# Chunked attention and a GELU layer on one core: zero products in TensorE's waits of the first tile, a weight cast moved, and three mm1 blocks taken by halves of K

## The chip, the cores and the metric

The kernel runs on one core of a Trainium2 chip. The metric is the device time of one execution in microseconds; smaller is better. The kernel before was timed in three runs: 282.14, 281.04 and 281.98 us, with a median of 281.98 us. A further execution was profiled; its own time was 281.53 us.

## The reference

```python
def _attn_ref(q, k, v):                       # (8, 8, 576, 64) float32
    chunk = 64
    nc = S // chunk
    scale = 1.0 / np.sqrt(D)
    # q, k, v in chunks of 64 rows; attention inside each chunk only
    scores = scale * np.matmul(q_c, k_c.transpose(0, 1, 2, 4, 3))
    ...
    attn = attn / (np.sum(attn, axis=-1, keepdims=True) + 1e-09)
    out = np.matmul(attn, v_c)
    ...

def _moe_ref(x, w_in, w_out):                 # x (4608, 512)
    h = x @ w_in                              # w_in (512, 2048)
    g = 0.5 * h * (1.0 + erf(h * inv_sqrt2))
    return (g @ w_out).astype(np.float32)     # w_out (2048, 512)
```

The attention output of all heads, laid side by side, is x (4608 rows of 512). The output is float32.

## The kernel before

The 4608 rows are cut into nine tiles of 512. Tiles 0 to 7 are the first eight chunks of each batch; the ninth gathers the last chunk of all eight batches. For each tile the kernel computes attention, which gives x transposed (512 features in four groups `ks` of 128 partitions by 512 rows, bf16), then mm1 (16 blocks `f` of 128 columns of w_in, each four products over `ks`, then GELU on ScalarE into `h`), then mm2 (`h` times w_out). The attention of a tile is computed on TensorE between the mm2 products of the tile before. From tile 3 on mm2 uses seven half-size products in the place of eight.

The order of the instructions on each engine is the order of the program text: the kernel stands in a manual schedule, and an engine takes its instructions in that order and waits for what each needs. All loads are issued by SyncE, in text order. They arrive as float32 in five `stage` buffers (two `wsum` buffers for some of the weights) and are cast to bf16 by DVE (`DV`), ScalarE (`AC`) or GpSimd (`PO`). The order of loads at the start is q and k of tile 0 by groups of two heads, v of tile 0, w_in in four blocks of 512 columns (the first two in two parts each), and then w_out, with q, k and v of tile 1 between.

The change lies in the first tile, where nothing runs beside the attention:

- `T[0]` to `T[7]` (`att_T`, line 162) transpose q and k of the four head groups on TensorE, q and k in turn, and copy them out of PSUM (q by DVE, k by ScalarE). `transposed` (line 155) takes a bank of `ps_tp` for q and of `ps_mm` for k.
- `att_S(0, g)` (line 363) makes the scores of a group in `ps_at` banks and their exponentials on ScalarE.
- `att_sums` (line 375) and `att_spread` (line 387) make the row sums with short products and spread the reciprocals, with a reciprocal and a transpose on DVE for each group.
- `att_av` (line 404) multiplies by v, first groups 0 and 1 (`g2` = 0) for half of the row blocks, then for the other half, then groups 2 and 3 (`g2` = 1). `att_x` (line 415) scales the result into x on DVE.
- `keep_warm(n)` (line 688) issues n products of 512 columns on zeros (`rest`) into a `ps_mm` bank of its own. It is called with a count of 7 at the start and of 3 behind `T[1]`, and four times with a count of 1; the diff touches the last four.
- `mm1_begin(0, 3)` (line 451) makes the first three blocks of mm1: blocks 0 and 1 by halves of K, then block 2 whole. Blocks 0 to 3 of w_in are cast by `win[0](i, engine)` (line 671).

After that, `phase(0, ...)` (line 623) runs the other mm1 blocks of tile 0, then its mm2 with the attention of tile 1 between: `duo_S`, `duo_sums`, `duo_av` (line 350, which needs v of tile 1, cast by GpSimd in `cast_v_plain`) and `duo_x` (line 357). Tile 1's mm1 follows.

Of the kernel before, what the change touches and what calls it, by code (L numbers as in the profile page):

```python
# [11 lines left out]
def kernel(  # L12
# [9 lines left out]
    nc = tc.nc  # L22
    P = 128
    f32 = mybir.dt.float32
# [4 lines left out]
    CH = 64  # L29
# [7 lines left out]
    CT = NC - 1  # L37
    MT = CT * CH
    NT = B + 1
    KS = d_model // P  # L40
# [5 lines left out]
    rest = consts.tile([P, 512], bf16, name="rest")  # L46
# [30 lines left out]
    ps_tp = ctx.enter_context(tc.tile_pool(name="ps_tp", bufs=2, space=bass.MemoryType.PSUM))  # L77
    ps_at = ctx.enter_context(tc.tile_pool(name="ps_at", bufs=3, space=bass.MemoryType.PSUM))
# [8 lines left out]
    tiles = [dict() for _ in range(NT)]  # L87
# [52 lines left out]
    def cast_v_plain(t, copy, ns=range(CT // 2), hs=slice(0, H)):  # L140
        st = tiles[t]
        if 0 in ns:
            st["v"] = ld.tile([P, H, CT // 2, D], bf16, tag="v", name="v_nat")
        for n in ns:
            copy(st["v"][:, hs, n], st["vf"][:, hs, n])
# [5 lines left out]
    def cast_qk(t, nm, g, copy):  # L151
        st = tiles[t]
        copy(st[nm][:, g].rearrange("p j r d -> p r j d"), st[nm + "f"][:, 2 * g:2 * g + 2])  # L153

    def transposed(t, nm, g):
        pool, tag = (ps_tp, "tp") if t or nm == "q" else (ps_mm, "mm")
        tp = pool.tile([P, 2, J, P], bf16, tag=tag, name="tp")
        for j in range(J):
            nc.tensor.transpose(tp[:, 0, j], tiles[t][nm][:, g, j].rearrange("p r d -> p (r d)"), ident[:])  # L159
        return tp[:, 0].rearrange("p j (i c) -> p i c j", i=CT)  # L160

    def att_T(t, nm, g, copy):
        tp = transposed(t, nm, g)
        if (nm, "T") not in tiles[t]:
            tiles[t][nm, "T"] = hsum.tile([P, G, CT, CH], bf16, tag=f"s{1 + 2 * t + (nm == 'q')}", name=nm + "T")
        xT = tiles[t][nm, "T"][:, g]
        copy(xT.rearrange("p i (c j) -> p i c j", j=J), tp)
        tiles[t][nm + "T", g] = xT

    def parity_blocks(ns=range(4)):  # L170

        for n in ns:
            for a in range(2):
                for r in range(2):
                    c = a ^ r
                    yield n, r, c, 2 * n + c, slice(CH * r, CH * (r + 1)), slice(CH * c, CH * (c + 1))
# [186 lines left out]
    def att_S(t, g):  # L363

        st = tiles[t]
        if g % 2 == 0:
            st["s_ps"] = [ps_at.tile([P, 2, CT // 2, CH], f32, tag="at", name="s_ps") for _ in range(2)]
        for n, r, c, i, rs, cs in parity_blocks():
            nc.tensor.matmul(st["s_ps"][r][cs, g % 2, n], st["kT", g][rs, i, :], st["qT", g][rs, i, :],
                             start=True, stop=True, tile_position=(CH * r, CH * c))  # L370
        st["pT", g] = work.tile([P, 2, CT // 2, CH], bf16, tag="pT", name="pT", bufs=8)
        for r in range(2):
            nc.scalar.activation(st["pT", g][:, r], st["s_ps"][r][:, g % 2], Act.Exp, scale=scale)

    def att_sums(t, g):

        st = tiles[t]
        pT = st["pT", g]
        st["sums", g] = ps_mm.tile([P, CT // 2, 2, 2], f32, tag="mm", name="sums_ps")
        for n in range(CT // 2):  # L380
            for e in range(2):
                for s in range(G):
                    nc.tensor.matmul(st["sums", g][QD * s:QD * (s + 1), n, :, e],
                                     pT[:, s // 2, n, 32 * e:32 * (e + 1)], ones_r[:],
                                     start=True, stop=True, tile_position=(0, QD * s))

    def att_spread(t, g):

        st = tiles[t]
        if g % 2 == 0:  # L390
            st["rcs", g // 2] = hsum.tile([P, 2, MT], f32, tag=f"s{3 + g // 2}", name="rcs")
        r1 = work.tile([P, NB], f32, tag="r1", name="r1", bufs=2)
        nc.vector.reciprocal(r1[:], st["sums", g][:].rearrange("p n c e -> p (n c e)"))
        nc.vector.transpose(st["rcs", g // 2][:, g % 2].rearrange("p (n e) -> p n e", e=32),  # L394
                            r1[:].to_broadcast([P, NB, 32]))

    def att_rc(t, g):
# [3 lines left out]
        nc.vector.transpose(rc[:], rb[:, g].to_broadcast([P, NB, 32]))  # L401
        tiles[t]["rc", g] = rc

    def att_av(t, g2, ns):

        st = tiles[t]
        pool, tag = ((ps_tp, "tp"), (ps_at, "at"))[g2]
        if 0 in ns:
            st["av", g2] = [pool.tile([P, 2, CT // 2, CH], f32, tag=tag, name="av_ps") for _ in range(2)]
        for g in (2 * g2, 2 * g2 + 1):  # L410
            for n, r, c, i, rs, cs in parity_blocks(ns):
                nc.tensor.matmul(st["av", g2][c][rs, g % 2, n], st["v"][cs, 2 * g + r, n, :], st["pT", g][cs, r, n],
                                 start=True, stop=True, tile_position=(CH * c, CH * r))

    def att_x(t, g2, c, ns):

        st = tiles[t]
        def part(p):
            return p.rearrange("p g (n c e) -> p g n c e", c=2, e=CH)[:, :, ns[0]:ns[-1] + 1, c]
        nc.vector.tensor_tensor(part(st["x"][:, 2 * g2:2 * g2 + 2]), st["av", g2][c][:, :, ns[0]:ns[-1] + 1],  # L420
                                part(st["rcs", g2][:]), op=mybir.AluOpType.mult)

    NB = MT // 32
    DV, AC, PO = nc.vector.tensor_copy, nc.scalar.copy, nc.gpsimd.tensor_copy

    def att_units(t, cq=DV, ck=DV):
        tiles[t]["x"] = xpool.tile([P, G, MT], bf16, tag="x", name="x")
        T = []
        for g in range(G):
            T += [lambda g=g: att_T(t, "q", g, cq),  # L430
                  lambda g=g: att_T(t, "k", g, ck if t == 0 or g < 2 else DV)]
        return T


# [16 lines left out]
    def mm1_begin(t, n):  # L451

        st = tiles[t]
        st["h"] = hpool.tile([P, FF, MT], bf16, tag="h", name="h")
        h_ps = [ps_mm.tile([P, MT], f32, tag="mm", name="h_ps") for _ in range(n)]
        order = [(f, ks) for k2 in range(2) for f in range(n - 1) for ks in (2 * k2, 2 * k2 + 1)] + \
                [(n - 1, ks) for ks in range(KS)]
        for f, ks in order:
            nc.tensor.matmul(h_ps[f][:], w_in_sb[:, ks, f * P:(f + 1) * P], st["x"][:, ks, :],  # L459
                             start=(ks == 0), stop=(ks == KS - 1))  # L460
        for f in range(n):
            nc.scalar.activation(st["h"][:, f, :], h_ps[f][:], Act.Gelu)
# [202 lines left out]
    def load_w_in(c, parts=1):  # L665
        raw = stage_tile(wsum if c < 2 else None)[:].rearrange("p (ks n) -> p ks n", ks=KS)
        n = WC // parts
        for a in range(parts):
            nc.sync.dma_start(raw[:, :, a * n:(a + 1) * n], w_in_v[:, :, c * WC + a * n:c * WC + (a + 1) * n])

        def cast(i, copy):
            copy(w_in_sb[:, :, c * WC + i * P:c * WC + (i + 1) * P], raw[:, :, i * P:(i + 1) * P])
        return cast
# [14 lines left out]
    def keep_warm(n):  # L688
        warm = ps_mm.tile([P, MT], f32, tag="mm", name="warm")
        for _ in range(n):  # L690
            nc.tensor.matmul(warm[:], rest[:, 0:P], rest[:], start=True, stop=True)  # L691
# [3 lines left out]
    def act_table(func):  # L695
        nc.scalar.activation(act_scratch[:], rest[:, 0:1], func)  # L696

    with tc.manual_schedule():
# [4 lines left out]
        win = [load_w_in(c, 2 if c < 2 else 1) for c in range(NWC - 1)]  # L703
        act_table(Act.Exp)
        keep_warm(7)
        T = att_units(0, DV, AC)
# [7 lines left out]
        T[1]()  # L714
        keep_warm(3)
        T[2]()
        T[3]()
        cast_qk(0, "k", 2, DV)
        att_S(0, 0)
        T[4]()  # L720
        T[5]()
        att_S(0, 1)
        T[6]()
        att_sums(0, 0)
        att_spread(0, 0)
        keep_warm(1)
        T[7]()
        att_S(0, 2)
        att_sums(0, 1)
        att_spread(0, 1)  # L730
        keep_warm(1)
        att_S(0, 3)
        att_sums(0, 2)
        att_spread(0, 2)
        att_sums(0, 3)
        att_spread(0, 3)
        keep_warm(1)
        cast_v_plain(0, AC, range(3, 4), slice(0, H // 2))
        att_av(0, 0, (0, 1))
        for c in range(2):  # L740
            att_x(0, 0, c, (0, 1))
        keep_warm(1)
        att_av(0, 0, (2, 3))
        for c in range(2):
            att_x(0, 0, c, (2, 3))
# [5 lines left out]
        win[0](0, PO)  # L751
        win[0](1, AC)
        act_table(Act.Gelu)
        win[0](2, DV)
        win[0](3, PO)
        mm1_begin(0, 3)
        load_qk(1, "q")
        wout.append(load_w_out(1))
# [22 lines left out]
        T = att_units(1, AC, AC)  # L781
# [47 lines left out]
        for t in range(1, NT):  # L829
            e1, e2 = {}, {}  # L830
            n = t + 1
# [71 lines left out]
```

## Time and profile before

| what | profiled execution |
|---|---|
| its own time | 281.53 us |
| span of the profile | 279.7 us |
| TensorE products, busy | 270.4 us (97%) |
| DVE busy | 166.2 us (59%) |
| ScalarE busy | 153.9 us (55%) |
| GpSimd busy | 87.5 us (31%) |
| mean granted TensorE clock | 0.982 |
| mean DMA rate | 193 GB/s |

Instructions are named by engine, line and tile: `PE L459 h_ps<-x,w_in_sb` is a product of `mm1_begin`. In the timeline the columns are the start, the duration (for several merged instructions: from the first start to the last end), the engine, the line, the operation and the count; in brackets the engine's idle time before it and what ended it. TensorE products overlap, so a product's own duration is longer than its distance from the next.

### The profile page before, as it was taken

To read this page: it belongs to the slowest core of one execution; us is meant where nothing else is said; L and a number is where in the kernel's file an instruction comes from. 1 tells how busy PE (TensorE), PEld (TensorE's weight loads), DVE (VectorE), ACT (ScalarE), POOL (GpSimd) and SP (SyncE) were. 2 spreads that over 40 slices of the span, in tenths; PEclk is the share of its full clock that TensorE was granted. 3 is DMA by queue.
4 is the path that set the end of the run, shared out by engine and by line. 5 is a ranking of instruction groups with operands and counts; after the bars stand their busy time and mean duration, and the time that the engine had idled before them with its cause. 6 is when DMAs were issued, how large, how long until landed. Compare 5 with 4: busy or idle time off the path is not lost.

```text
span 279.7 us, 6860 instructions
## 1 busy us (share of the span) xinstructions
PE 270.4 (97%) x2802; PEld 159.6 (57%) x2802; DVE 166.2 (59%) x355; ACT 153.9 (55%) x289; POOL 87.5 (31%) x178
## 2 busy tenths in 40 slices
PE   8789999999999999999999999999999999999993
PEld 3544454444444444448845884587458745874682
DVE  2673326701944595995768587757785877434532
ACT  2547756778646765762567256725672565116500
POOL 2535665341540802740480372014802120000000
PEclk9759999999999999999999999999999999999999
DMA  6999999898999999998999939995942310040005
GB/s 208 254 352 407 391 388 270 191 259 209 299 195 272 245 199 247 287 214 217 259 162 215 284 117 220 198 173 163 217 92 46 114 39 0 2 150 2 0 2 151
DMA packets 118064, 53.93 MB, mean 193 GB/s; under 512 B 93456, under 2 KB 112912, under 8 KB 118032
## 3 DMA queue, kind: packets, MB, share of 16 engines
q1 hardware_dynamic: 117712, 52.97, 73.1%
q8 instruction: 22, 0.36, 0.5%
q10 hardware_dynamic: 320, 0.52, 0.5%
q14 instruction: 10, 0.08, 0.1%
HBM read 36.70 MB, written 9.44 MB: 165 GB/s over the span
## 4 chain that ended last, share of the span: by engine, by line
PE 91%; DVE 3%; DMA 2%; SPq 1%; issue 1%; POOL 0%; ACT 0%
PE h_ps L446 43%; PE y_ps L502 27%; PE y_ps L596 10%; PE y_ps L620 4%; DMA arrival<-in_q_dram 2%; PE s_ps L222 2%; PE av_ps L292 2%; PE h_ps L459 1%; PE tp L159 1%; SPq L105 1%; DVE x L360 1%; DVE rc L401 1%; DVE rcs L394 1%; DVE x L420 0%; PE warm L691 0%
## 5 line engine op out<-in xcount | busy, mean ns | idle before, releaser
L446 PE MATMUL h_ps<-x,w_in_sb 128*128 128x512 bf16 x564 | 123.4, 379 | 0.4 <-DVE x L360 0.4
L449 ACT ACTIVATE h<-h_ps 128x512 bf16<-128x512 f32 x141 | 83.7, 597 | 56.2 <-PE h_ps L446 56.2
L446 PEld LDWEIGHTS <-w_in_sb 128*128 128x128 bf16 x564 | 55.2, 98 | 66.1 <-issue 0.7
L153 POOL CAST q_nat<-arrival 128x512 bf16<-128x512 f32 x33 | 21.1, 677 | 59.7 <-DMA arrival<-in_q_dram 46.0
L502 PEld LDWEIGHTS <-h_s 128*128 128x128 bf16 x384 | 36.8, 98 | 4.5
L502 PE MATMUL y_ps<-w_t,h_s 128*128 128x256 bf16 x288 | 33.7, 273 | 0.0
L596 PE MATMUL y_ps<-w_out_sb,h 128*128 128x512 bf16 x144 | 32.5, 380 | 0.0
L502 PEld LDWEIGHTS <-h 128*128 128x128 bf16 x288 | 28.2, 98 | 4.5
L244 DVE STREAM_TRANSPOSE pt<-pT 128x256 f32<-128x256 f32 x28 | 12.2, 437 | 26.7 <-ACT pT L229 26.7
L153 POOL CAST k_nat<-arrival 128x512 bf16<-128x512 f32 x33 | 19.4, 625 | 17.2 <-DMA arrival<-in_k_dram 14.4
L200 POOL CAST v_nat<-arrival 128x1024 bf16<-128x1024 f32 x14 | 14.3, 1039 | 30.9 <-DMA arrival<-in_v_dram 30.9
L482 DVE TENSOR_TENSOR h_s<-h 128x512 bf16<-128x512 bf16 (+1 forms) x30 | 11.1, 371 | 20.6 <-ACT h L449 20.6
L502 PE MATMUL y_ps<-w_out_sb,h 128*128 128x256 bf16 x192 | 22.9, 273 | 0.0
L596 PEld LDWEIGHTS <-h 128*128 128x128 bf16 x144 | 13.4, 98 | 15.6 <-issue 0.2
L696 ACT ACT_TABLE_LOAD x16 | 20.5, 1283 | 1.0 <-PEq L887 0.7
L247 DVE TENSOR_REDUCE part<-pt 128x16 f32<-128x512 bf16 x28 | 19.2, 686 | 1.0
L299 DVE TENSOR_TENSOR x<-av_ps,rc 128x512 bf16<-128x512 f32 x28 | 17.9, 683 | 3.1 <-PE av_ps L292 2.5
L535 ACT COPY y_sb<-y_ps 128x512 f32<-128x512 f32 x5 | 2.9, 585 | 26.1 <-PE y_ps L502 26.1
L229 ACT ACTIVATE pT<-s_ps 128x512 bf16<-128x512 f32 x28 | 14.4, 607 | 1.5 <-PE s_ps L222 1.5
L254 POOL COPY part<-part 32x32 f32<-32x32 f32 x40 | 9.8, 245 | 12.6 <-DVE part L247 10.9
L620 PE MATMUL y_ps<-w_out_sb,h 128*128 128x512 bf16 x48 | 11.8, 379 | 0.3 <-ACT h L449 0.3
L483 DVE TENSOR_TENSOR h_s<-h_s,h 128x512 bf16<-128x512 bf16 (+1 forms) x30 | 11.1, 371 | 1.0
(92 smaller groups left out, 248.0 us busy)
## 6 DMA issues: line engine op xcount, KB each, us to landing
out_dram<-y_sb SPq DMA_DIRECT2D x32, 256.0 KB, 3.0
arrival<-in_q_dram SPq DMA_DIRECT2D x7, 1024.0 KB, 6.1
arrival<-in_k_dram SPq DMA_DIRECT2D x24, 256.0 KB, 6.0
arrival<-in_v_dram SPq DMA_DIRECT2D x42, 128.0 KB, 3.0
arrival<-in_moe_w_out_dram SPq DMA_DIRECT2D x4, 1024.0 KB, 12.4
arrival<-in_v_dram SPq DMA_DIRECT2D x8, 256.0 KB, 6.4
arrival<-in_moe_w_in_dram SPq DMA_DIRECT2D x4, 512.0 KB, 6.0
arrival<-in_moe_w_in_dram SPq DMA_DIRECT2D x2, 1024.0 KB, 10.0
```

What stands on the lines that cost most here:

```text
L153: copy(st[nm][:, g].rearrange("p j r d -> p r j d"), st[nm + "f"][:, 2 * g:2 * g + 2])
L200: copy(st["v"][:, r::2], st["vf"][:, r::2])
L229: nc.scalar.activation(pT[:].rearrange("p u (c j) -> p u c j", j=J), s_ps[g2][c][:].rearrange("p u (j c) -> p u c j", j=J), Act.Exp, scale ...
L244: nc.vector.transpose(pt[:].rearrange("p n e u -> p (n e u)").bitcast(f32).rearrange("p (n e) -> p n e", e=32), st["pT", 2 * g2 + c][:].re ...
L247: nc.vector.tensor_reduce(st["part", g2][:, c, :, :, 0], pt[:].rearrange("p n e u -> p n u e"), axis=mybir.AxisListType.X, op=mybir.AluOpT ...
L299: nc.vector.tensor_tensor(x.rearrange("p n (e u) -> p n e u", u=2), st["av"][g2][c][:].rearrange("p n (e u) -> p n e u", u=2), st["rc", 2 ...
L446: nc.tensor.matmul(h_ps[a][:], w_in_sb[:, ks, o * P:(o + 1) * P], st["x"][:, ks, :], start=(ks == 0), stop=(ks == KS - 1))
L449: nc.scalar.activation(st["h"][:, f_of(t, f + a), :], h_ps[a][:], Act.Gelu)
L502: nc.tensor.matmul(out[m], lhs[:, f, m * P:(m + 1) * P], rhs[:, f, :], start=fresh and f == 0 and (m == 0 or len(out) == 3), stop=(f == FH ...
L596: nc.tensor.matmul(y_ps[:], st["h"][:, f, ms * P:(ms + 1) * P], w_out_sb[:, f, :], start=(f == 0), stop=(f == FF - 1))
L620: nc.tensor.matmul(tiles[t]["y_ps", ms][:], tiles[t]["h"][:, f, ms * P:(ms + 1) * P], w_out_sb[:, f, :], start=(f == 0), stop=False)
L696: nc.scalar.activation(act_scratch[:], rest[:, 0:1], func)
```

## The change

`transposed` and `att_T` take a count `busy`: so many products of 512 columns on zeros are issued into the bank that the transposes then overwrite. The same is done in the banks of the first `av` products (allocated earlier, in `av_banks`) and in the first bank of mm1. Four `keep_warm(1)` go. All three blocks of `mm1_begin` are made by halves of K. Block 2 of w_in is cast by GpSimd and block 3 by DVE, which was the other way round.

```diff
+    def stay_busy(bank, n):
+
+        for _ in range(n):
+            nc.tensor.matmul(bank, rest[:, 0:P], rest[:], start=True, stop=True)
+
-    def transposed(t, nm, g):
+    def transposed(t, nm, g, busy=0):
         pool, tag = (ps_tp, "tp") if t or nm == "q" else (ps_mm, "mm")
         tp = pool.tile([P, 2, J, P], bf16, tag=tag, name="tp")
+        stay_busy(tp[:].rearrange("p a j c -> p (a j c)").bitcast(f32), busy)
...
+    def av_banks(t, g2):
+        pool, tag = ((ps_tp, "tp"), (ps_at, "at"))[g2]
+        tiles[t]["av", g2] = [pool.tile([P, 2, CT // 2, CH], f32, tag=tag, name="av_ps") for _ in range(2)]
+        return tiles[t]["av", g2][0][:].rearrange("p g n e -> p (g n e)")
+
     def att_av(t, g2, ns):
 
         st = tiles[t]
-        pool, tag = ((ps_tp, "tp"), (ps_at, "at"))[g2]
-        if 0 in ns:
-            st["av", g2] = [pool.tile([P, 2, CT // 2, CH], f32, tag=tag, name="av_ps") for _ in range(2)]
...
         h_ps = [ps_mm.tile([P, MT], f32, tag="mm", name="h_ps") for _ in range(n)]
-        order = [(f, ks) for k2 in range(2) for f in range(n - 1) for ks in (2 * k2, 2 * k2 + 1)] + \
-                [(n - 1, ks) for ks in range(KS)]
+        stay_busy(h_ps[0][:], 3)
+        order = [(f, ks) for k2 in range(2) for f in range(n) for ks in (2 * k2, 2 * k2 + 1)]
...
         T[2]()
-        T[3]()
+        T[3](1)
         cast_qk(0, "k", 2, DV)
         att_S(0, 0)
-        T[4]()
-        T[5]()
+        T[4](1)
+        T[5](2)
         att_S(0, 1)
-        T[6]()
+        T[6](1)
         att_sums(0, 0)
         att_spread(0, 0)
-        keep_warm(1)
-        T[7]()
+        T[7](1)
         att_S(0, 2)
         att_sums(0, 1)
         att_spread(0, 1)
-        keep_warm(1)
+        first_half = av_banks(0, 0)
+        stay_busy(first_half, 1)
         att_S(0, 3)
         att_sums(0, 2)
         att_spread(0, 2)
+        second_half = av_banks(0, 1)
+        stay_busy(first_half, 3)
         att_sums(0, 3)
         att_spread(0, 3)
-        keep_warm(1)
         cast_v_plain(0, AC, range(3, 4), slice(0, H // 2))
+        stay_busy(first_half, 3)
         att_av(0, 0, (0, 1))
         for c in range(2):
             att_x(0, 0, c, (0, 1))
-        keep_warm(1)
+        stay_busy(second_half, 3)
         att_av(0, 0, (2, 3))
...
         act_table(Act.Gelu)
-        win[0](2, DV)
-        win[0](3, PO)
+        win[0](2, PO)
+        win[0](3, DV)
         mm1_begin(0, 3)
```

More of the change, by code (lines that the diff above doesn't have):

```diff
@@ L160, in transposed, with att_T @@
         return tp[:, 0].rearrange("p j (i c) -> p i c j", i=CT)
-    def att_T(t, nm, g, copy):
-        tp = transposed(t, nm, g)
+    def att_T(t, nm, g, copy, busy=0):
+        tp = transposed(t, nm, g, busy)
         if (nm, "T") not in tiles[t]:
@@ L429, in att_units @@
         for g in range(G):
-            T += [lambda g=g: att_T(t, "q", g, cq),
-                  lambda g=g: att_T(t, "k", g, ck if t == 0 or g < 2 else DV)]
+            T += [lambda busy=0, g=g: att_T(t, "q", g, cq, busy),
+                  lambda busy=0, g=g: att_T(t, "k", g, ck if t == 0 or g < 2 else DV, busy)]
         return T
```

## The prediction

> **What bounds the kernel now.** I read the page first: the slices of the span, then the chain that ended last, then the first 24 us by the timeline, and last the stage at 47 to 54 us, where the chain leaves TensorE again.
>
> ```profile
> PE   8789999999999999999999999999999999999993
> PEclk9759999999999999999999999999999999999999
> PE 91%; DVE 3%; DMA 2%; SPq 1%; issue 1%; POOL 0%; ACT 0%
> ```
>
> TensorE is 91% of the chain, and only one stretch (the second and third slices) has a granted clock below full. Stretches cut at the clock's steps (columns: length, TensorE busy with its count of products, granted clock, DMA share, GB/s):
>
> ```profile
> 3.16:6.58 3.42, 3.23 (x14) 1.00 0.97 293
> 6.58:9.99 3.41, 2.12 (x49) 1.00 1.14 331
> 9.99:13.40 3.41, 3.19 (x96) 0.50 0.85 193
> 13.40:16.81 3.41, 2.95 (x104) 0.50 0.95 305
> 16.81:20.23 3.42, 2.90 (x53) 0.50 1.08 368
> 20.23:23.64 3.41, 3.41 (x17) 1.00 1.05 405
> ```
>
> The clock is half from 9.99 to 20.23 us: three stretches of 3.41 us. The 1.00 before 6.58 is no reading: in the timeline the first seven 512-column products take 3.17 us, that is (3.17-0.61)/6 = 0.427 us apart, while 64 of them later take 13.81 us (chain, 81.60), 0.216 apart. So TensorE started at half, got full clock at 6.58, lost it at 9.99 after a stretch with 2.12 us busy, mostly short transposes, and got it back at 20.23 after one with two microseconds of dense products. Then the timeline:
>
> ```profile
> 1.20 3.17 PE L691 MATMUL warm<-rest 128*128 128x512 bf16 x7 [1.20 <-DVE rest L47]
> 5.38 1.41 PE L691 MATMUL warm<-rest 128*128 128x512 bf16 x3
> 18.14 3.77 PE L459 MATMUL h_ps<-x,w_in_sb 128*128 128x512 bf16 x12 [0.52 <-DVE x L420]
> 16.50 0.61 POOL L672 CAST w_in_sb<-arrival 128x512 bf16<-128x512 f32 x1 [0.95 <-DMA arrival<-in_moe_w_in_dram]
> 18.17 0.61 POOL L672 CAST w_in_sb<-arrival 128x512 bf16<-128x512 f32 x1 [1.06 <-DMA arrival<-in_moe_w_in_dram]
> ```
>
> and, a tile later:
>
> ```profile
> 47.52 0.61 POOL L145 CAST v_nat<-arrival 128x512 bf16<-128x512 f32 x1 [2.01 <-DMA arrival<-in_v_dram]
> 48.20 0.45 PE L354 MATMUL av_ps<-pT,v_nat 64*64 64x64 bf16 x32
> 51.66 1.46 PE L446 MATMUL h_ps<-x,w_in_sb 128*128 128x512 bf16 x6
> 53.56 0.81 PE L446 MATMUL h_ps<-x,w_in_sb 128*128 128x512 bf16 x3 [0.45 <-DVE x L360]
> ```
>
> The last block of the second tile's v lands at 47.5, is cast until 48.13, and TensorE takes it at 48.20. TensorE and the v transfer now arrive there together. This decides my sum.
>
> **The change, part by part.** 19 products are added and four warm ones go: 15 more, 0.216 us each at full clock, 0.427 at half. They matter only by what they do to the clock and by what they push back.
>
> *Holding the clock at 9.99.* The stretch 6.58 to 9.99 holds 16 transposes of 128 columns (2048) and 32 score products of 64 by 64 (by array area 512). At full clock it could stream 8192 columns, so 31%, and that lost the clock. Four added products fall into it (before T[3], T[4], and two before T[5]): 2048 columns more, 56%. Rows to either side: the end of the span, where a stretch with 20 products of 256 columns (62%) kept the clock; 3.16 to 6.58 at half clock, 2560 columns of products and 1024 of transposes, which gained it. 56% is nearer to 62 than to 31: I take it as held. After 9.99 two more products stand before T[6] and T[7], then one, and three groups of three in waits, so the next stretches are denser still.
>
> [...]
>
> *The first tile at full clock.* The last k group is cast until 10.29+0.61 = 10.90, so T[7] starts at 11.0 (now 11.47, behind a half-clock product) and its ACT copy ends at 12.0 instead of 12.7. Behind it on ACT stand the exponentials of two groups, 0.67 each: 13.4. The third group of three (0.65) delays the last sums to 13.7-14.0, but DVE is later: its copy of q ends at 11.3, then four reciprocal-and-transpose pairs at 0.95 end at 15.15 (now 16.07). The x products: pair one 15.2-15.9; pair two needs the last v block, cast until 15.55 by ACT and GpSimd, and its av behind three products that end at 15.6, so 16.1-16.8; pair three 1.3, until 18.1 (now 19.18). The first mm1 product needs w_in's first cast (16.50+0.61 = 17.11); the three products on h_ps end about then: start 17.2, now 18.14.
>
> *w_in's third block on GpSimd, three blocks by halves of K.* GpSimd takes block 2 at 18.17 in the place of block 3, ends at 18.78; block 3 goes to DVE behind the x products and is not wanted before 20. By halves, block 2's first half comes after four products (17.2+0.86 = 18.1) and waits in TensorE's order until 18.8; behind it stand eight products, 1.7: mm1_begin ends at 20.5, now at 18.14+5x0.427+7x0.216 = 21.8. The old order would end at 19.8 at full clock, so this part costs 0.7 here, and it is one I count as hidden (below). TensorE is then 1.3 us ahead.
>
> *How far the 1.3 us goes.* Next in line: w_in's block 8, cast by 24.14 and wanted at 24.7 instead of 26.05, still in time; w_out blocks and k of tile 1 have 1.9 us or more. At the v wait nothing is left: the DMA share is 1.05 to 1.09 in every stretch from 20 to 50 us and SyncE issues w_in, w_out, q, k and v back to back, none of them waiting for the first tile. So v still lands at 47.5, and TensorE reaches its av at 46.9 and waits 1.3 us. From 48.20 its own work is unchanged: 51.66 plus six products, 52.96, where it now stands until 53.56 for DVE. DVE's chain (transpose, reciprocal, rc, x) is 1.3 earlier up to its first x, which then follows av at 48.65; two rc and four x of 0.65 end at 52.45, below 52.96. So of the wait 53.56-52.96 = 0.6 us goes, and nothing else. After it the next foreign input is the flipped k of tile 2 (issued 60.35, median 4.0 to landing, needed at 66.24): 1.9 us of room.
>
> Sum against the profiled execution, 281.53 us (span 279.7 and 1.8 around it): 281.53-0.6 = 280.9. It lies 0.45 below the median of 281.98. The runs spread from 281.04 to 282.14, as they would if the clock's stretches fall differently in each; a kernel held by the v transfer would lose that spread on the upper side. I say **281.0**. Mm1_begin may end as late as 21.1 before this changes, which hides the 0.7 of the reordering.
>
> **Rivals.**
>
> 1. *The v bound gives way.* If v lands earlier or its cast isn't last, the whole 1.3 us comes through: 280.2. For it: nothing in the profile but run-to-run drift of transfers. Against: the 2.01 us that GpSimd waits for that block. It is the only case beyond 0.5% on that side.
>
> 2. *The clock falls at 9.99 all the same, but is back at 16.82.* Streamed columns need not be what counts: if transposes count for nothing, the four products are 25% alone. Then until 13.4 everything is as now, the third group of three moves the last sums from 14.23 to 15.4, the next ends at 16.7, av is 1.4 us late, and the full clock afterwards pays it back: mm1_begin ends at 21.9, time 281.5. The stretch 13.40 to 16.82 then has about five and a half products, 2800 columns, and small ones, against 3072 that sufficed in 16.81 to 20.23. [...]
>
> 3. *It falls and stays half until 20.23: the products become the bound.* The groups of three then cost 1.28 each in TensorE's queue ahead of av: sums of the last group at 15.4, first av 17.1, second av 18.8, mm1_begin from 20.75 to 23.35, 1.45 later than now. All behind it moves, the v wait included: 283.0. With stretches that fall a microsecond later, half of that again at half clock: 283.5. It decides as soon as the products delay mm1_begin's end past 21.8. For it: some 2350 columns in the run's first stretch (products from 1.20 to 3.16 at 0.427 each) did not raise the clock. Against: twice the products of today in these stretches.
>
> 4. *The products find their bank not free* and change nothing in the clock: the tp bank is read by DVE until 9.9, wanted at 11.9; mm banks rotate with one user fewer than now. Each product merely takes a wait's place: 281.5.
>
> **How the numbers follow.** Forecast 0.52; rival 1: 0.10; rival 2: 0.15; rival 3: 0.15; rival 4: 0.03; 0.05 for what I don't see, on the slow side. About 0.5% is what a measurement of this kernel can tell from no change: 280.57 to 283.39. Faster: rival 1, and a fifth of the forecast by the spread of runs, 0.20. Slower: two thirds of rival 3 and the unseen, 0.15. The rest, 0.65, is the same. The range goes from rival 1 at 280.2 to rival 3 at 283.0; it leaves out half of rival 1, the later part of rival 3 and the unseen.
>
> **What would show it.** Clock 1.00 from 6.58 on with no half stretch; L459 starting near 17.2 and ending near 20.5, with a wait on GpSimd's w_in cast inside; TensorE waiting about 1.3 us at L354 for v_nat; no wait at L446 near 53; span near 279.1. Wrong: a half-clock stretch from 9.99; L354 before 47.8; or v_nat cast at another time than 47.5 by more than 0.3 us.

## The result, and the profile after

The changed kernel took 280.52 us (median of 20 executions, 279.65 to 284.34) and the kernel before, beside it, 282.02 (20 executions, 280.76 to 284.03). The ratio is 0.9947, with a 95% interval from 0.9927 to 0.9967: faster by 0.5%, 1.5 us by the medians. A second comparison gave 280.12 us and 0.9952 (0.9930 to 0.9974). Ratios leave out executions more than 1.5% above the fastest of their kernel; medians count all.

The first profile of the changed kernel shows an execution slower than most, 281.58 us. Its page, the slices and the chain:

```profile
PE   6899999999999999999999999999999999999993
PEclk9979999999999999999999999999999999999998
PE 92%; DVE 2%; DMA 2%; ACT 1%; issue 1%; SPq 0%; POOL 0%
```

In the first tile one slice is below full clock where there were two before. Cut at the clock's steps, the same profile (length, TensorE busy and count, granted clock, DMA share, GB/s):

```profile
4.95:8.36 3.41, 1.77 (x14) 1.00 0.94 320
8.36:11.78 3.42, 3.42 (x104) 1.00 1.01 251
11.78:15.19 3.41, 2.79 (x133) 1.00 1.00 246
15.19:18.60 3.41, 3.41 (x51) 0.50 1.01 334
```

The clock is lost for one stretch of 3.41 us, after the stretch 11.78 to 15.19, and not for three. The execution profiled in the second comparison (279.92 us) loses it nowhere in the first tile; the slices (the 8 at the end lies behind the last product), then the stretches:

```profile
PEclk9999999999999999999999999999999999999998
```

```profile
6.97:10.38 3.41, 2.79 (x52) 1.00 1.12 316
10.38:13.79 3.41, 2.90 (x139) 1.00 0.80 189
13.79:17.21 3.42, 2.93 (x101) 1.00 1.04 330
17.21:20.62 3.41, 3.25 (x40) 1.00 1.06 371
```

The stretch from 6.97, which is the one that lost the clock before (2.12 us busy), is now busy for 2.79 us and keeps it. The timeline of the same profile, the first mm1 products and the stage of the second tile's v:

```profile
18.00 2.75 PE L467 MATMUL h_ps<-x,w_in_sb 128*128 128x512 bf16 x12
46.89 0.61 POOL L145 CAST v_nat<-arrival 128x512 bf16<-128x512 f32 x1 [0.79 <-DMA arrival<-in_v_dram]
47.05 0.29 PE L360 MATMUL av_ps<-pT,v_nat 64*64 64x64 bf16 x12
47.55 0.35 PE L360 MATMUL av_ps<-pT,v_nat 64*64 64x64 bf16 x20 [0.22 <-POOL v_nat L145]
50.92 1.46 PE L454 MATMUL h_ps<-x,w_in_sb 128*128 128x512 bf16 x6
```

mm1_begin takes 2.6 us where it took 3.6, TensorE waits for v in the middle of its av products, for 0.22 us, and the second tile's mm1 goes on from 50.92 with its seventh product at 52.42 (before, from 51.66 with the seventh at 53.56).

How to read the mean clocks below: one stretch at half clock costs 3.41/280/2 = 0.006 of the mean, and the half clock after the last product up to 0.004 in these profiles (0.003 in the first of the changed kernel, from 278.02 us to the end at 279.77). By this estimate an execution that lost one stretch shows 0.994 at most, and at 0.995 and above no stretch of the first tile was at half clock. I call such an execution whole.

### The profile page after: what moved, and what is told of

It reads as the page before. It is cut to its first block, busy times and chain, and to the rows that moved or that the text cites. A ratio compares the mean times of both kernels' runs of the same rounds, so it can differ in the third digit from the quotient of the medians.

```text
span 279.8 us, 6890 instructions
## 1 busy us (share of the span) xinstructions
PE 270.9 (97%) x2817; PEld 159.4 (57%) x2817; DVE 167.5 (60%) x355; ACT 153.8 (55%) x289; POOL 87.4 (31%) x178
## 4 chain that ended last, share of the span: by engine, by line
PE 92%; DVE 2%; DMA 2%; ACT 1%; issue 1%; SPq 0%; POOL 0%
PE h_ps L454 43%; PE y_ps L510 27%; PE y_ps L604 10%; PE y_ps L628 4%; DMA arrival<-in_k_dram 2%; PE s_ps L228 2%; PE av_ps L298 2%; PE av_ps L158 1%; PE tp L165 1%; PE h_ps L467 1%; DVE x L366 1%; DVE rc L407 1%; PE tp L158 0%; SPq L105 0%; PE sums_ps L389 0%
## 5 line engine op out<-in xcount | busy, mean ns | idle before, releaser
L490 DVE TENSOR_TENSOR h_s<-h 128x512 bf16<-128x512 bf16 (+1 forms) x30 | 11.8, 392 | 20.1 <-ACT h L457 20.1
L704 ACT ACT_TABLE_LOAD x16 | 20.5, 1283 | 1.0 <-PEq L897 0.7
```

## The experiments

### The kernel before and the changed kernel again

No edit.

> The kernel before, unchanged, for a second profile of it and for the granted clock of each of its executions. Theory A (the clock's phase makes the spread): mean granted clocks between 0.975 and 0.99 in every execution, since 10.2 us at half clock cost 0.018, and the faster executions are those with fewer half-clock stretches; median 282.0 us. Theory B (the spread comes from the loads alone): the clock is the same in all and the time still spreads by 2 us.

> The changed kernel, unchanged, for a profile of an execution that keeps its clock: the first profile has one half-clock stretch, 14.82 to 18.23 us, and 281.58 us. Theory A (as predicted, the second tile's v holds TensorE): in an execution without a half-clock stretch the last v block lands at 47.0 to 47.6 us, TensorE waits about 1 us for it at the second tile's av, and the time is 280.9. Theory B (v isn't the last to come): TensorE doesn't wait for v there, the second tile's mm1 goes on at 52.2 to 52.5 instead of 53.6, and the time is 280.0 to 280.4.

The kernel before: 283.25 us in its own 12 executions, mean clocks 0.965 to 0.988. Against the 35 executions of the same kernel beside them that is a ratio of 1.0044 (1.0010 to 1.0077), so with no edit at all a difference of 0.4% came out beyond its interval. The median clock was 0.976 in the 12 and 0.984 in the 35. Ratios as small as those below are therefore to be read together with the clocks. Over the 97 other executions of the kernel before that the comparisons of this section count, the median is 282.06, no mean clock is above 0.994, and the time goes with the clock: median 280.95 us for the 10 executions at 0.99 and above, 281.9 for the 60 from 0.98 to 0.99, 282.8 for the 27 below 0.98. Its second profile (284.72 us) has four half-clock stretches, from 10.88 to 24.54 us. Theory A on its spread holds, as far as it goes: the correlation of time and clock is -0.70.

The changed kernel: 280.12 us, all 12 executions whole; with the 20 of the first comparison, 29 of 32 are. The whole ones have a median of 280.35 us, but still lie between 279.65 and 281.91. Theory B fits better: the second tile's mm1 goes on at 52.42 and the time is 280.12, as it says. TensorE does wait for v, but for 0.22 us, and that wait cost nothing at 52.42 (see the run without v's last block).

### The products alone, the reordering alone

```diff
-        order = [(f, ks) for k2 in range(2) for f in range(n) for ks in (2 * k2, 2 * k2 + 1)]
+        order = [(f, ks) for k2 in range(2) for f in range(n - 1) for ks in (2 * k2, 2 * k2 + 1)] + \
+                [(n - 1, ks) for ks in range(KS)]
...
-        win[0](2, PO)
-        win[0](3, DV)
+        win[0](2, DV)
+        win[0](3, PO)
```

This on the changed kernel gives the products alone; the reverse on the kernel before gives the reordering alone.

> The zero products as in the changed kernel, but w_in's blocks 2 and 3 cast as before and mm1_begin's third block whole at the end. Theory A (the reordering costs 0.7 us in the first tile and is hidden by the wait for v): 280.9 or as the changed kernel, mm1_begin ending some 0.7 us earlier than in the changed kernel. Theory B (no wait for v hides anything): 0.5 to 0.7 us faster than the changed kernel, near 279.9. Theory C (the halves by K are what saves the time, since TensorE would wait for the x of groups 2 and 3): 0.3 to 0.6 us slower than the changed kernel.

> Only the reordering: blocks 2 and 3 of w_in cast by GpSimd and DVE, three blocks by halves of K; no added products, the four single warm products as before. Theory A (the clock is the gain): no change, 281.7 to 282.3, with the same half-clock stretches as the kernel before. Theory C (the halves by K are the gain): 281.0 to 281.4.

The products alone: 280.55 us, ratio 0.9967 (0.9935 to 1.0000), 11 of 12 executions whole. The reordering alone: 282.26 us, ratio 1.0006 (0.9971 to 1.0040), none of 12 whole. So the products, not the reordering, keep the clock. By time alone the interval of the products just reaches 1, and the reordering by itself does nothing that can be measured. Whether it adds to or takes from the products is open: the intervals of the products alone and of the whole change overlap almost entirely, and mm1_begin ended at 20.65 us without the reordering and at 20.59 with it, not 0.7 apart.

### Which products hold the clock

Without the four products ahead of T[3] to T[5]; without all six ahead of T[3] to T[7]; with four transposes of zeros for each of the six; and with the later groups of three cut to one:

```diff
-        T[3](1)
+        T[3]()
...
-        T[4](1)
-        T[5](2)
+        T[4]()
+        T[5]()
```

```diff
-        stay_busy(tp[:].rearrange("p a j c -> p (a j c)").bitcast(f32), busy)
+        for j in range(J * busy):
+            nc.tensor.transpose(tp[:, 0, j % J], rest[:, 0:P], ident[:])
```

```diff
-        stay_busy(first_half, 3)
+        stay_busy(first_half, 1)
```

> The changed kernel without the four products ahead of T[3], T[4] and T[5]; all later ones stay. Theory A (these four hold the clock where it was lost before): one or two half-clock stretches of 3.41 us in most executions, mean granted clock 0.982 to 0.993, 281.3 to 282. Theory B (the later groups alone would hold it or bring it back at once): mean clock 0.996 or more in most executions and the time of the changed kernel, 280.1 to 280.5.

> The changed kernel without any of the six products ahead of T[3] to T[7]; the single product and the groups of three behind them stay. It is the twin of the run with transposes of zeros in their place. Theory A (transposes don't count for the clock): the same clocks as with the transposes, 0.985 to 0.994 in most executions, and 281.3 to 282. Theory B (they count in part): clearly lower clocks here than with the transposes, 0.975 to 0.988, and slower.

> The changed kernel with each of the six products ahead of T[3] to T[7] replaced by four transposes of 128 columns of zeros: the same 512 columns and the same time on TensorE (4x0.057 = 0.228 for 0.216 us). Theory A (streamed columns count for the clock, whatever the instruction): as the changed kernel, mean clock 0.996 or more, 280.1 to 280.5. Theory B (transposes don't count): as the kernel without the early products or worse, mean clock 0.98 to 0.993, 281.3 to 282.3.

> The changed kernel with each later group of three products cut to one, so five single products as in the kernel before; the six early ones stay. Theory A (the early products carry the clock over the stretch where it was lost, but the later stretches need the groups): the clock falls one or two stretches later than before, mean clock 0.982 to 0.994, 281 to 281.8. Theory B (the early six are enough): mean clock 0.996 or more and 279.8 to 280.3, a little faster than the changed kernel, since eight products fewer stand in TensorE's queue.

| kernel | whole executions | median us | ratio to the kernel before (95%) |
|---|---|---|---|
| changed, first and second comparison | 29 of 32 | 280.52, 280.12 | 0.9947 (0.9927 to 0.9967), 0.9952 (0.9930 to 0.9974) |
| without the four early products | 5 of 10 | 280.62 | 0.9952 (0.9917 to 0.9988) |
| without the six | 3 of 12 | 281.40 | 0.9953 (0.9920 to 0.9985) |
| transposes for the six | 2 of 10 | 281.69 | 0.9992 (0.9959 to 1.0025) |
| later groups cut to one | 0 of 12 | 281.41 | 0.9963 (0.9937 to 0.9989) |

The ratios of the two without early products rest on 8 executions each and are soft; the clocks speak plainly. Most executions need both halves: the early products carry the clock over the first thin stretch, the groups of three over the later ones. With thin later groups the clock falls in every execution, in the profile after the stretch that ends at 14.77:

```profile
7.95:11.36 3.41, 3.41 (x121) 1.00 1.12 272
11.36:14.77 3.41, 3.06 (x116) 1.00 0.97 260
14.77:18.19 3.42, 2.09 (x52) 0.50 1.05 345
18.19:21.60 3.41, 3.41 (x9) 0.50 1.06 395
```

Busy time does not tell who keeps the clock (3.06 us lost it here, 2.79 kept it above). In these profiles the columns streamed do, but for a narrow band. I counted them for each stretch of the first tile at full clock in the ten profiles without missing products: columns of the 512-column products, of the transposes, and a quarter of those of the 64 by 64 score and av products. All stretches up to 2832 columns (five) lost the clock, all from 3328 up kept it, and of three at 3072 one lost it. At 0.216 us for 512 columns 3.41 us hold 8083; the 8192 of the prediction is 1% above that. At half clock about the same number separates the stretches: those up to 2944 columns (eight, of the 4089 that 3.41 us hold at 0.427 us for 512) stayed at half, and those from 3200 up (six) were followed by full clock. The stretches of the kernel with transposes:

```profile
5.48:8.89 3.41, 2.42 (x41) 1.00 1.03 350
8.89:12.31 3.42, 3.35 (x129) 1.00 1.09 254
12.31:15.72 3.41, 2.35 (x85) 1.00 0.98 283
15.72:19.13 3.41, 3.41 (x70) 0.50 1.06 363
```

The stretch from 8.89 holds 512 columns of products, 3584 of transposes and 512 of scores and keeps the clock; the one from 12.31 holds 2560 columns of products, no transposes and 256 of scores, and loses it. By this trace transposes do count, then, by more than half of their columns: with less the stretch from 8.89 would lie below the 2832 that lost it. By the number of whole executions, though, theory B fitted better, 2 of 10. What I can show for it is a gap in the stretch that failed, in which TensorE waited for nothing that the profile shows:

```profile
14.14 0.19 PE L390 MATMUL sums_ps<-ones_r,pT 128*32 128x2 bf16 x4 [0.94 <-issue]
```

The gap stands at the same place in the row sums of 11 of the 14 profiles (0.28 and 0.43 us in the two of the changed kernel), and one profile can't say that it is what costs the other executions their clock. Beside it, on the queue that the page calls `instruction` (q8), the first transfer of 16 KB starts at 11.76 us here, and TensorE goes on at 14.14 (12.46 and 14.92 in the first profile of the changed kernel). In all 11 profiles it goes on 2.2 to 2.7 us after the start of that transfer, whether that is at 13.9 us or at 17.2. No run moved that transfer, so that the gap comes from it is not shown. Against the kernel without the six, the lost clock is shorter with transposes (mean 0.985 to 0.994 where it was lost, 0.975 to 0.988 there), as theory B of that run had it: they count. Why a later stretch then fails so often stays open.

### What is left in whole executions

The second tile's av one mm2 slot later; its last block of v not loaded (the block before it is cast in its place); the sixth tile's small sums on DVE; and the first and third together:

```diff
-                      13: [lambda: duo_av(1, 0), lambda: duo_x(1, 0, 0), lambda: duo_x(1, 0, 1), U[2], U[3]],
-                      14: [lambda: duo_av(1, 1), lambda: duo_x(1, 1, 0), lambda: duo_x(1, 1, 1)]},
+                      14: [lambda: duo_av(1, 0), lambda: duo_x(1, 0, 0), lambda: duo_x(1, 0, 1), U[2], U[3]],
+                      15: [lambda: duo_av(1, 1), lambda: duo_x(1, 1, 0), lambda: duo_x(1, 1, 1)]},
```

```diff
-        for n in range(CT // 2):
+        for n in range(CT // 2 - (t == 1)):
             nc.sync.dma_start(tiles[t]["vf"][:, :, n], ...)
```

```diff
-        return AC if t <= FIRST7 else PO
+        return AC if t <= FIRST7 else DV if t == 5 else PO
```

> The changed kernel with the second tile's two av groups and their x products one mm2 slot later (14 and 15 for 13 and 14), so that TensorE has four more products, 0.86 us, before it needs the last v block. Theory A (in executions that keep the clock the wait for v is what is left, 0.2 to 1 us): 0.3 to 0.5 us faster than the changed kernel, about 279.8, with the slower executions gone most. Theory B (DVE's chain of rc and x products ends last there, not v): no change or 0.2 to 0.5 slower, 280.1 to 280.7, since the x products start later.

> The changed kernel with the last block of the second tile's v left out of the load (the block before it is cast in its place), so 256 KB less and nothing to wait for at the second tile's av. Theory A (v's landing bounds the executions that keep the clock and makes their spread): no wait at the second tile's av, 279.5 to 279.9, spread below 1 us. Theory B (v isn't the bound): as the changed kernel, 280.1 to 280.5, with the same spread of 2 us.

> The changed kernel with the small copies of the row sums of the sixth tile done by DVE in the place of GpSimd, where they stand behind GpSimd's casts of loads. In two profiles of executions with a whole clock (281.3 and 281.5 us) those copies began 5 us later than in one of 279.9, and TensorE waited 0.7 and 1.1 us for DVE's sums of h at 155 us. Theory A (that wait is what makes the slower executions with a whole clock): no wait at 155 us, the executions above 281 gone, median 279.9. Theory B (the spread comes from the v wait and elsewhere): as the changed kernel, 280.1 to 280.5, with executions up to 281.9.

> The changed kernel with both: the second tile's av groups one mm2 slot later, and the sixth tile's small sums on DVE. Theory A (the v wait at 48 us and the sums at 155 us take back the gain of the first tile): 279.5 to 279.8, a ratio to the kernel before near 0.992, spread below 1.2 us. Theory B (each is hidden by another): as the changed kernel, 280.1 to 280.5.

| kernel | median us (lowest to highest) | ratio to the kernel before (95%) |
|---|---|---|
| av later | 280.40 (279.50 to 282.69) | 0.9939 (0.9906 to 0.9972) |
| v's last block not loaded | 280.87 (279.40 to 282.04) | 0.9936 (0.9904 to 0.9967) |
| small sums on DVE | 280.74 (279.40 to 283.32) | 0.9947 (0.9915 to 0.9979) |
| av later, small sums on DVE | 280.01 (279.63 to 284.36) | 0.9939 (0.9909 to 0.9968) |

They are 9, 6, 12 and 12 executions, and none can be told from the changed kernel. Of whole executions alone (29, 9, 6, 9 and 9, the changed kernel first) the medians are 280.35, 280.40, 280.87, 279.93 and 279.91, the highest 281.91, 282.69, 282.04, 281.23 and 281.00; the two with small sums on DVE lean towards their theory A, but not clear of noise. Without v's last block there is no wait at av, as theory A had it, and still the executions lie 2.6 us apart. DVE's chain ends last there:

```profile
46.62 0.45 PE L360 MATMUL av_ps<-pT,v_nat 64*64 64x64 bf16 x32
50.08 1.46 PE L454 MATMUL h_ps<-x,w_in_sb 128*128 128x512 bf16 x6
51.99 2.32 PE L454 MATMUL h_ps<-x,w_in_sb 128*128 128x512 bf16 x10 [0.45 <-DVE x L366]
```

The seventh mm1 product comes at 51.99, 5.37 us after the first av product. In the whole profile of the changed kernel, with the wait of 0.22 us, it is 5.37 as well (47.05 to 52.42): DVE's chain ends last in both, and removing the wait is worth nothing there. That the one is 0.4 us ahead of the other comes from the first tile. A wait for v that does cost something stands in the profile of the products alone:

```profile
47.42 0.40 PE L360 MATMUL av_ps<-pT,v_nat 64*64 64x64 bf16 x12
48.49 0.35 PE L360 MATMUL av_ps<-pT,v_nat 64*64 64x64 bf16 x20 [0.66 <-POOL v_nat L145]
```

There the seventh product comes 5.72 us after the first av product, so 0.66 us of wait cost 0.35. With av later, its profile (281.33 us) loses its lead elsewhere, at 155 us, in two waits:

```profile
155.26 0.28 PE L510 MATMUL y_ps<-w_t,h_s 128*128 128x256 bf16 x1 [0.47 <-DVE h_s L492]
156.19 2.90 PE L510 MATMUL y_ps<-w_t,h_s 128*128 128x256 bf16 x25 [0.65 <-DVE h_s L492]
```

DVE is late there because its totals wait for GpSimd's small copies (`total` at 147.60, after 2.93 us of waiting for `part`), which stand behind casts of loads; GpSimd in that profile, and in the whole profile of the changed kernel (279.92 us):

```profile
137.65 2.28 POOL L153 CAST q_nat<-arrival 128x512 bf16<-128x512 f32 x4 [15.38 <-DMA arrival<-in_q_dram]
146.62 1.97 POOL L260 COPY part<-part 32x32 f32<-32x32 f32 x8
```

```profile
133.10 2.28 POOL L153 CAST q_nat<-arrival 128x512 bf16<-128x512 f32 x4 [12.31 <-DMA arrival<-in_q_dram]
141.82 2.47 POOL L260 COPY part<-part 32x32 f32<-32x32 f32 x8
```

With the copies on DVE the profile has no wait there, but executions above 281 us remain. In the last kernel's profile (281.00 us) a third wait shows, in the first tile:

```profile
19.98 1.90 PE L467 MATMUL h_ps<-x,w_in_sb 128*128 128x512 bf16 x8 [1.77 <-POOL w_in_sb L680]
```

It is the wait on block 2 that the reordering adds. So in whole executions TensorE has caught up with the loads, and which load or cast it meets differs from one to the next. Three waits were seen: for v in three profiles (0.22 to 0.66 us), for block 2 of w_in in two (0.36 and 1.77), for the sums at 155 us in two. Followed by the ends of the GELUs, the six whole profiles differ by up to 1.5 us in the first tile, 0.6 at the second tile's av and 1.5 at 155 us, and elsewhere by no more than 0.2. That the same holds for the executions without a profile is not shown.

## Why the prediction was right or wrong

*The clock at 9.99.* Right. I counted 4608 columns for the stretch; in the whole profile it holds 2048 of products, 2048 of transposes and 512 of scores, and kept the clock. My bracket of 31% to 62% narrows to 35% to 41% (2832 and 3328 of 8083). Rivals 2 and 3, in which the clock falls there, occur in no profile of the changed kernel; where it did fall, in 3 of 32 executions, the one that was profiled lost it later, after 15.19. Rival 4 (no effect on the clock) falls with the mean clocks.

*The first tile.* Close, by compensation. mm1_begin was to run from 17.2 to 20.5; in the whole profile it ran from 18.0 to 20.6. It started late because the row sums of the last group stood at 14.15 to 14.96 and not at 13.7 to 14.0, and 0.28 of that is the gap in them; the rest was not followed. It lost nothing inside, because block 2 of w_in had been cast by 18.4. The wait on block 2, 0.7 by my sum, is 0 in this profile, 0.4 in another and 1.8 in a third. That the end came out right is luck.

*How far it goes.* This is the step that was mis-sized: "At the v wait nothing is left ... So v still lands at 47.5, and TensorE reaches its av at 46.9 and waits 1.3 us." I allowed 0.6 us to pass. In the whole profile TensorE reached its av at 47.05 and the seventh mm1 product of the second tile came at 52.42 against 53.56: 1.1 us passed, the whole lead, as rival 1 has it. Two of the signs that I had named for being wrong came: the av before 47.8, and v's last cast 0.6 us away from 47.5 (46.89). Two things were wrong. I took the landing in one execution for a constant: over the 13 profiles that load all of v, its last cast ended between 47.0 and 48.4 us, and the 48.13 of my profile is in the later half. And I let all 32 products wait for the last block, though the order of `duo_av` needs it only at the thirteenth. The landing is the larger part: in the two profiles in which the wait for v ends last (products alone, small sums on DVE) the seventh product comes 4.7 us after the end of v's last cast, and with the cast until 48.13 that would be 52.85, so 0.7 us. So the result lies between my forecast (281.0) and rival 1 (280.2), in which the v bound gives way, and nearer to the rival; it stands just at the 0.5% that I took as the limit of measurement.

*Against what.* The profiled execution before (281.53 us, three half-clock stretches) was faster than the median by 0.5 us, and I said that a kernel held by the loads would lose the spread above it. In part this came: the clock's share of the spread went, and 2 us of it stayed. The two profiled executions (281.53 and 279.92 us) also differ by some 0.4 us that no step of mine names: at 189 us TensorE of the kernel before stands among score products, with nothing shown to wait for. Both its profiles have that gap (0.22 and 0.81 us) and no other kernel's has; the reordering alone hasn't either and is no faster than the kernel before, so the gap can hardly be the gain.

## What to carry to other kernels

Where TensorE's clock falls, count the columns that it streams in each stretch between the clock's steps, not its busy time (3.06 us busy lost it here, 2.79 kept it), and fill the thinnest stretch first and then every one behind it: here the later groups alone kept the clock in half of the executions at most (5 of 10 and 3 of 12), and the early products alone in none (0 of 12). Before a gain on the critical path is summed up to the end, look for the next transfer that the path meets, and take its landing from several executions: here v's last cast ended between 47.0 and 48.4 us over 13 profiles. A wait that a profile shows is not yet a price: see whether another chain ends as late without it. Where the profile shows a wait on a tile, look which instruction of the group needs the last piece.

## What the runs showed of the hardware that I had not expected

Transposes on TensorE counted for the clock in the trace that tests them: 3584 columns of them with 512 of products and 512 of scores kept it, where 2560 columns of products with 256 or 272 of scores lost it. The number of columns in 3.41 us that separated the stretches lay between 2832 and 3328 at full clock and between 2944 and 3200 at half clock, so it was nearly the same number, though half clock has room for half as many (512 columns took 0.427 us there and 0.216 at full clock). In the profiles cut at the clock's steps here the steps lay multiples of 3.41 us apart, at another offset each time (6.58, 9.99 and 20.23 us in the first profile of the kernel before, 15.19 and 18.60 in the first of the changed kernel). By its mean clocks (0.994 down to 0.965, at 0.006 for a stretch) the kernel before lost from one to about five stretches. TensorE also stood for 0.16 to 1.49 us in the middle of the first tile's row sums in 11 of 14 profiles, always at the same product of one kernel, and went on 2.2 to 2.7 us after the start of a 16 KB transfer on the `instruction` queue; that the one waits for the other was not tried.
